# The output projection's first weight piece, cut in halves around the last values, in a decode attention kernel

## Chip, cores and metric

The kernel runs on one core of one Trainium2 chip. The metric is device time in microseconds (us) of one execution. Beside it stands one execution recorded by the hardware profiler; its span runs from the first to the last profiled instruction of the program.

## What is computed

One decode step for two tokens (B = 2, D = 512): a layer norm, grouped attention over the last 4096 positions of a cache, an output projection with `wo`, and a gate from a small gated MLP.

```python
xn = _layernorm(x)
# attention: 32 query heads, 8 key/value heads, Dh = 128, W = 4096
q = (xn @ wq).reshape(B, 1, 32, 128).transpose(0, 2, 1, 3)
k = repeat(k_cache[:, :, Sk - W:, :], 4, axis=1)
v = repeat(v_cache[:, :, Sk - W:, :], 4, axis=1)
p = softmax(einsum("bhqd,bhkd->bhqk", q, k) * Dh ** -0.5)
o = einsum("bhqk,bhkd->bhqd", p, v)
s = o.transpose(0, 2, 1, 3).reshape(B, 1, 4096) @ wo        # wo is 4096 x 512
# gate: gMLP with w_in, w_sp, b_sp, w_out
g = silu(_B_ref(xn, w_in, w_sp, b_sp, w_out))
return x + s * g
```

Everything is fp32. Nearly all of the time goes into reading the window of both caches (32 MB each, eight loads of 4 MB), `wq` and `wo` (8 MB each) and `w_in`.

## The kernel before

The 16 pairs of token and key/value head are worked on as eight **units** `u` = 0 to 7, each with two heads: units 0 to 3 belong to token 0, units 4 to 7 to token 1. A unit's keys `K:u` and values `V:u` are 4 MB each. Every load is issued on SP's queue. VectorE transposes the keys in eight turns (`T:u.q`); TensorE multiplies them with the queries (`shares`, `scores`), in two halves `a`; VectorE and ScalarE make the softmax (`rowmax`, `mg`, `bias`, `exp`, `probs_t`); TensorE multiplies the probabilities with the values (`pv:u.a`, which needs `V:u`), ScalarE evacuates (`evac`), TensorE and VectorE bring the heads into columns (`col`, `gather`).

The output projection takes three **sets** of heads, `SETS`: set 0 is key/value heads 0 to 3 (16 blocks of `wo`, 4 MB), set 1 is heads 4 and 5 (8 blocks, 2 MB), set 2 is heads 6 and 7 (8 blocks, 2 MB). A block is 128 rows by 512 columns of `wo`. Set 0 is complete when units 0, 1, 4 and 5 are gathered, set 1 after unit 6, set 2 after unit 7. `spread:i` (TensorE) and `oT:i` (VectorE, function `place`) turn a set's values into the stationary operand `oT_i`.

The blocks are multiplied in two ways. The first 28 blocks go through `wo_early`: 128 x 512 matmuls, one of four column groups of the array each, summed in the PSUM tile `part`; each fp32 matmul shows in the profile as two passes. ScalarE then copies `part` to SBUF (`parts`) and four small matmuls (`pz`, function `add_parts`) add its four groups into `so`. The last four blocks go through `wo_last`, straight into `so`, as four 128 x 128 matmuls each. VectorE multiplies `so` with the gate, adds `x`, and SP writes the output.

The order of all this is written out by hand in the string `ORDER`: each name is one step, taken from left to right, and each engine gets its instructions in that order. A step on an engine therefore stands behind all earlier steps of that engine, whatever they wait for. The loads `K`, `V`, `wo` stand in the same string and set the order of SP's queue. They go into a ring of four 4 MB buffers (`slot`), so a load is issued once the buffer's former content has been used: in the kernel before, `V:7` follows keys 6 (`T:6.7`), `wo:0` follows values 5 (`pv:5.1`), `wo:1` follows keys 7 (`T:7.7`).

In the kernel before, `wo:0` is one transfer of 4 MB. `wo:1` is one buffer filled by five transfers: 2 MB of set 1, then set 2 as 1 MB, 512 KB, 256 KB and 256 KB. In `ORDER`, `X:n` is two blocks of set 0, `Y:n` two blocks of set 1, `U:n` two of the first four blocks of set 2, and `Z:0`, `Z:1`, `Z:2` are the last 2, 1 and 1 blocks.

Of the kernel before, what the change touches and what calls it, by code (L numbers as in the profile page):

```python
# [9 lines left out]
F32 = mybir.dt.float32  # L10
# [4 lines left out]
P = 128  # L15
# [28 lines left out]
scores:5.1 evac:4 col:4 rowmax:5.0  # L44
K:7 V:6 T:6.0 rowmax:5.1 mg:5 T:6.1 T:6.2 shmax:5 bias:5 T:6.3 exp:5.0 T:6.4 exp:5.1 T:6.5 probs_t:5.0 shares:6.0
keep:6.0 lsum:5 shsum:5 scores:6.0 probs_t:5.1 T:6.6 T:6.7 rowmax:6.0 pv:5.0 weights:5 shares:6.1 keep:6.1 pv:5.1
V:7 T:7.0 wo:0 scores:6.1 rowmax:6.1 T:7.1 T:7.2 mg:6 T:7.3 shmax:6 bias:6 T:7.4 evac:5 col:5 exp:6.0 exp:6.1 T:7.5
probs_t:6.0 T:7.6 T:7.7 wo:1 lsum:6 shares:7.0 keep:7.0 pv:6.0 scores:7.0 shares:7.1 rowmax:7.0 keep:7.1 shsum:6
scores:7.1 probs_t:6.1 weights:6 rowmax:7.1 mg:7 pv:6.1 evac:6 shmax:7 gather:5 col:6 bias:7 exp:7.0 gather:6 exp:7.1
probs_t:7.0 spread:0 probs_t:7.1 lsum:7 spread:1 pv:7.0 shsum:7 oT:0 weights:7 pv:7.1 X:0.6 X:0.0 oT:1 X:0.2 X:0.4  # L50
evac:7 X:0.3 col:7 X:0.7 gather:7 spread:2 X:0.5 Y:0.1 Y:0.0 Y:0.3 X:0.1 Y:0.2 oT:2 U:0.0 U:0.1 parts:0 Z:0 pz:0 Z:1 Z:2
"""


# [16 lines left out]
def kernel(  # L71
# [14 lines left out]
    pe, dve, act, sp = (InOrder(tc, e) for e in (nc.tensor, nc.vector, nc.scalar, nc.sync))  # L86
    B, _, D = x.shape
# [11 lines left out]
    DC = D // G  # L99
# [9 lines left out]
    ps = ctx.enter_context(tc.tile_pool(name="ps", bufs=1, space=bass.MemoryType.PSUM))  # L109

    def slot(name, *shape):
        return ring.tile([P, *shape], F32, tag="slot", name=name)

    def bank(name, *shape):
        return ps.tile([P, *shape], F32, tag="kt", name=name, bufs=2)
# [11 lines left out]
    for a in range(0, KT, 2):  # L127
        t = slot(f"wq{a}", 2, HQ * DH)
# [17 lines left out]
    def load(u, src, name):  # L146
        t = slot(f"{name}{u}", UJ, DH)
        b, v = divmod(u, HKV // 2)
        first = src[b, 2 * v, SK - W, :]
        of = bass.AP(tensor=src.tensor, offset=first.offset, ap=[[UJ * DH, P // 2], [SK * DH, 2], [1, UJ * DH]])  # L150
        sp.dma_start(t.rearrange("p j d -> p (j d)"), of)
        return t
# [17 lines left out]
    rowm = cst.tile([P, 32], F32, tag="rowm", name="rowm")  # L170
# [55 lines left out]
    for nj in (8, 16):  # L226
# [3 lines left out]
        at = cst.tile([P, nx], F32, tag=f"at{nj}", name=f"at{nj}")  # L230
# [7 lines left out]
    for n in range(G):  # L238
        pz = bank(f"z{n}", 512)[:, :FC]
        for k in range(KT):  # L240
            pe.matmul(
                pz[32 * k : 32 * k + 32, :], xnT[:, k, :], win[:, k, n * FC : (n + 1) * FC],
                start=True, stop=True,
# [31 lines left out]
    u = cst.tile([P, 2, FT, B], F32, tag="u", name="u")  # L275
# [37 lines left out]
    for j in range(FT):  # L313
        g = j % G
# [26 lines left out]
    def place_queries():  # L341
        dve.tensor_tensor(
            free_ap(qb, 16, [[REP, G], [32, NP * G], [1, REP]]), free_ap(qa, 0, [[0, G], [REP, NP * G], [1, REP]]),
            free_ap(grpm, 0, [[1, G], [0, NP * G], [0, REP]]), op=ALU.mult,
        )
# [3 lines left out]
    def silu():  # L349
        dve.tensor_scalar(gate, ys, -1.0, 80.0, op0=ALU.mult, op1=ALU.min)  # L350
        act.activation(gate, gate, AF.Exp)
        dve.tensor_scalar_add(gate, gate, 1.0)
        dve.reciprocal(gate, gate)
        dve.tensor_mul(gate, gate, ys)
# [10 lines left out]
    sets = {}  # L365
    for i, (kv, n, nj) in enumerate(SETS):
        o1 = cst.tile([P, B, 32], F32, tag=f"o1_{i}", name=f"o1_{i}")
        oT = cst.tile([P, nj, 32], F32, tag=f"oT_{i}", name=f"oT_{i}")
# [102 lines left out]
    col = {}  # L471
# [22 lines left out]
    def spread(i):  # L494
        o1, oT, nj = sets[f"oT{i}"]
        pts[i] = bank(f"oT_ps{i}", B, 32)
        pe.matmul(pts[i], perms[nj][0].rearrange("p h a x -> p (h a x)"), o1, start=True, stop=True)

    def place(i):
        _, oT, nj = sets[f"oT{i}"]  # L500
        nx = 32 // nj
        t = sb.tile([P, B, nx, nj], F32, tag="ot", name=f"ot{i}", bufs=1)
        dve.tensor_tensor(
            t, pts[i].rearrange("p b (x j) -> p b x j", x=nx), free_ap(perms[nj][1], 0, [[0, B], [1, nx], [0, nj]]),
            op=ALU.mult,
        )
        dve.tensor_reduce(
            oT[:, :, 0 : 16 * B : 16].rearrange("p j b -> p b j"), t.rearrange("p b x j -> p b j x"), axis=AX.X, op=ALU.add
        )


    wo_s = []
# [2 lines left out]
        wo_s.append(wo[r0:r1, :].rearrange("(p j) d -> p j d", j=nj))  # L515
    blocks = []

    def load_wo(n):
        t = slot(f"wo{n}", 16, D)
        a = 0  # L520
        for i in ((0,), (1, 2))[n]:
            for j, n in (((0, 16),), ((0, 8),), ((0, 4), (4, 2), (6, 1), (7, 1)))[i]:
                sp.dma_start(t[:, a : a + n, :], wo_s[i][:, j : j + n, :])
                blocks.append((t[:, a : a + n, :], sets[f"oT{i}"][1], j))
                a += n

    EARLY = 28
    done = 0
# [1 line left out]
    def wo_early(n, at):  # L530
        nonlocal done
        if done == 0:
            part.append(ps.tile([P, 512], F32, tag="s0", name="part"))
        t, oT, j = blocks[n]
        for a in range(at, at + 2):
            g = done % G
            pe.matmul(
                part[0][32 * g : 32 * g + 32, :], oT[:, j + a, :], t[:, a, :], start=(done < G), stop=(done >= EARLY - G)
            )
            done += 1  # L540

    part = []

    def copy_parts():
        parts.append(sb.tile([P, D], F32, tag="o", name="parts", bufs=1))
        act.activation(parts[0], part[0], AF.Copy)

    def wo_last(n):
        if n == 0:
            so.append(bank("so", DC))  # L550
        t, oT, j = blocks[3 + n]
        for a in range(t.shape[1]):
            for g in range(G):
                pe.matmul(
                    so[0][32 * g : 32 * g + 32, :], oT[:, j + a, :], t[:, a, g * DC : (g + 1) * DC],
                    start=(n == 0 and a == 0), stop=(j + a == oT.shape[1] - 1),
                )

    def add_parts():
        for g in range(G):  # L560
            pe.matmul(
                so[0][32 * g : 32 * g + 32, :], rowm, parts[0][:, g * DC : (g + 1) * DC], start=False, stop=False
            )

    parts, so = [], []
    STEPS = dict(
        T=turn, rowmax=row_max, mg=spread_max, shmax=share_max, bias=bias, exp=probs, probs_t=probs_t, lsum=own_sum,
        shsum=share_sum, weights=weights, shares=shares, keep=keep, scores=scores, pv=pv, evac=evacuate, col=collect,
        gather=gather,
    )  # L570

    def step(name, u, a=()):
        if name == "q":
            place_queries()
        elif name == "silu":
            silu()
        elif name == "K":
            units[u].k = load(u, k_cache, "k")
        elif name == "V":
            units[u].v = load(u, v_cache, "v")  # L580
        elif name == "wo":
            load_wo(u)
        elif name == "spread":
            spread(u)
        elif name == "oT":
            place(u)
        elif name == "X":
            wo_early(0, 2 * a[0])
        elif name == "Y":
            wo_early(1, 2 * a[0])  # L590
        elif name == "U":
            wo_early(2, 2 * a[0])
        elif name == "Z":
            wo_last(u)
        elif name == "parts":
            copy_parts()
        elif name == "pz":
            add_parts()
        else:
            STEPS[name](units[u], *a)  # L600
# [6 lines left out]
    for line in ORDER.strip().split("\n"):  # L607
        for name in line.split():
            name, at = name.split(":")
            u, _, a = at.partition(".")  # L610
            step(name, int(u), (int(a),) if a else ())
# [33 lines left out]
```

## Time and profile before

| | |
|---|---|
| median of 3 runs | 217.01 us (216.76 to 217.04) |
| the profiled execution's own time | 217.29 us |
| its span | 215.5 us |
| mean granted TensorE clock | 0.825 |
| TensorE matmul busy | 143.2 us (66%) |
| VectorE busy | 126.7 us (59%) |
| ScalarE busy | 51.6 us (24%) |
| read from memory | 89.40 MB, 415 GB/s over the span |

A busy share is the part of the span in which the engine had an instruction running; matmul ends are modelled, so TensorE's share is not its load at its peak. Lines of the profile name an engine (PE is TensorE's matmul, PEld its weight load, DVE VectorE, ACT ScalarE, SPq SyncE's queue), the operation, and its output and inputs by tile names. Nearly all instructions carry line 65, the helper that keeps program order, so they are told apart by tile: `acc` is `pv`, `sh` is `shares`, `part` is `wo_early`, `so` is `wo_last` and `add_parts`.

### The profile page before, as it was taken

Reading aid. Unit: us, or ns where it says so; the run is one execution under the profiler, and the core shown is the slowest. Engines: PE = TensorE matmul, PEld = TensorE weight load, DVE = VectorE, ACT = ScalarE, POOL = GpSimd, SP = SyncE. Lnnn points to the kernel's source line nnn. Section 1 sums busy time; section 2 is a strip of 40 time slices with the busy share of each in tenths; the row PEclk is TensorE's granted clock in tenths of the full one; section 3 lists DMA queues with packets and bytes.
Section 4 is the critical chain, followed back from the end, with each engine's and each line's share of the span. In section 5 each row is a group of like instructions: output and inputs, shape, how many; then the busy total and the mean of one; then the engine's idle time right before and its main releaser. Section 6 shows DMA issues by size and latency. Waiting matters only on the chain.

```text
span 215.5 us, 2332 instructions
## 1 busy us (share of the span) xinstructions
PE 143.2 (66%) x900; PEld 48.1 (22%) x900; DVE 126.7 (59%) x218; ACT 51.6 (24%) x129; POOL 4.5 (2%) x17
## 2 busy tenths in 40 slices
PE   0179796833854966964991795389259917987793
PEld 0117622111120221222220231123112201232231
DVE  2611213169899799649928972993698099636011
ACT  5011103300116036033330602142051206142201
POOL 8000000000000000000000000000000000000000
PEclk9999569665998896796697599669755997996999
DMA  7999999999999999999999999999999999999990
GB/s 246 432 443 444 398 429 465 414 458 414 456 408 447 420 426 444 426 443 426 450 420 450 408 441 420 426 450 426 447 415 456 401 456 414 447 426 417 420 374 22
DMA packets 3930, 89.54 MB, mean 416 GB/s; under 512 B 446, under 2 KB 462, under 8 KB 848
## 3 DMA queue, kind: packets, MB, share of 16 engines
q1 hardware_dynamic: 3900, 89.40, 96.8%
q8 instruction: 7, 0.11, 0.2%
q14 instruction: 3, 0.02, 0.0%
q10 hardware_dynamic: 20, 0.01, 0.0%
HBM read 89.40 MB, written 0.00 MB: 415 GB/s over the span
## 4 chain that ended last, share of the span: by engine, by line
DMA 63%; PE 23%; DVE 8%; ACT 3%; issue 1%; ACTq 0%
DMA v<-in_A_v_cache_dram 42%; DMA k<-in_A_k_cache_dram 16%; PE acc L65 10%; DMA win<-in_B_w_in_dram 5%; PE sh L65 5%; DVE kts L65 4%; PE part L65 4%; PE s L65 3%; DVE pT L65 1%; ACT p L65 1%; ACT o L65 1%; DVE gate L65 1%; PE mo L65 1%; ACT ss L65 1%; DVE qb L65 1%
## 5 line engine op out<-in xcount | busy, mean ns | idle before, releaser
L65 DVE STREAM_TRANSPOSE kts<-k 128x1024 f32<-128x1024 f32 x64 | 75.6, 1218 | 29.5 <-DMA k<-in_A_k_cache_dram 29.5
L65 PE MATMUL sh<-kts,qb 128*32 128x512 f32 x256 | 41.6, 775 | 13.2 <-DVE kts L65 9.3
L65 PE MATMUL acc<-v,pT 128*32 128x512 f32 x256 | 37.4, 707 | 8.8 <-DVE pT L65 4.4
L65 ACT ACTIVATE p<-s,nb 128x512 f32<-128x512 f32 x32 | 22.5, 733 | 36.2 <-DVE nb L65 36.2
L65 ACT ACTIVATE ss<-sh 128x512 f32<-128x512 f32 x16 | 9.6, 599 | 59.1 <-PE sh L65 59.1
L65 DVE STREAM_TRANSPOSE pT<-p 128x1024 f32<-128x1024 f32 x16 | 19.6, 1225 | 2.3 <-ACT p L65 2.1
L65 PE MATMUL s<-ss,sums 128*128 128x512 f32 x32 | 18.8, 671 | 2.3 <-ACT ss L65 2.3
L65 PE MATMUL mo<-mg,joint 128*128 128x16 f32 x16 | 4.0, 327 | 23.4 <-DVE mg L65 23.4
L65 PEld LDWEIGHTS acc<-v,pT 128*32 128x32 f32 x256 | 10.5, 145 | 35.1 <-issue 27.0
L65 PEld LDWEIGHTS sh<-kts,qb 128*32 128x32 f32 x256 | 8.8, 126 | 34.2 <-issue 28.8
L65 DVE TENSOR_REDUCE m<-s 128x1 f32<-128x512 f32 x16 | 10.7, 671 | 4.2 <-PE s L65 4.2
L65 PE MATMUL q_ps<-wq,xnT 128*32 128x512 f32 x64 | 10.5, 784 | 3.5 <-DMA wq<-in_A_wq_dram 3.5
L65 ACT ACTIVATE o<-acc,wd 128x128 f32<-128x128 f32 x32 | 9.1, 368 | 15.0 <-PE acc L65 15.0
L65 PEld LDWEIGHTS mo<-mg,joint 128*128 128x128 f32 x16 | 3.2, 250 | 27.2 <-DVE mg L65 24.4
L65 PE MATMUL z<-win,xnT 128*32 128x448 f32 x32 | 5.6, 869 | 4.7 <-DMA win<-in_B_w_in_dram 4.7
L65 PE MATMUL part<-wo,oT 128*32 128x512 f32 x56 | 7.7, 596 | 1.4 <-ACT o L65 1.4
L65 PEld LDWEIGHTS s<-ss,sums 128*128 128x128 f32 x32 | 5.0, 197 | 10.3 <-issue 7.7
L65 PE MATMUL zT_ps<-rowm,z 128*128 128x2 f32 x28 | 6.6, 370 | 0.0
L65 PEld LDWEIGHTS zT_ps<-rowm,z 128*128 128x128 f32 x28 | 6.5, 325 | 0.0
L65 ACT ACTIVATION_READ_ACCUMULATOR p<-s,nb 128x1 f32 x32 | 6.5, 203 | 0.0
L65 ACT ACT_TABLE_LOAD x4 | 5.1, 1283 | 2.6 <-POOL hT L164 2.6
L65 DVE COPY z<-z 128x448 f32<-128x448 f32 x2 | 1.3, 626 | 7.5 <-PE z L65 7.5
(111 smaller groups left out, 68.4 us busy)
## 6 DMA issues: line engine op xcount, KB each, us to landing
k<-in_A_k_cache_dram SPq DMA_DIRECT2D x8, 4096.0 KB, 27.4
v<-in_A_v_cache_dram SPq DMA_DIRECT2D x8, 4096.0 KB, 29.8
wq<-in_A_wq_dram SPq DMA_DIRECT2D x1, 4096.0 KB, 24.5
wq<-in_A_wq_dram SPq DMA_DIRECT2D x2, 2048.0 KB
wo<-in_A_wo_dram SPq DMA_DIRECT2D x1, 4096.0 KB, 30.4
win<-in_B_w_in_dram SPq DMA_DIRECT2D x1, 3584.0 KB, 11.5
wo<-in_A_wo_dram SPq DMA_DIRECT2D x1, 2048.0 KB
wout<-in_B_w_out_dram SPq DMA_DIRECT2D x1, 1792.0 KB, 15.3
```

The lines of the kernel that those rows point to most:

```text
L65: return self.tc.keep_in_program_order(call(*args, **kwargs))
```

## The change

The first piece of `wo` is loaded in two halves of 2 MB, one ahead of `V:7` and one behind it. Set 2 comes in three transfers (4, 3 and 1 blocks) in place of four (4, 2, 1, 1). The first half's eight blocks (`X:0.0` to `X:0.3`) now stand between `col:6` and `pv:7.0`; for that, `gather:5`, `spread:0` and `oT:0` are moved ahead. The second half's eight blocks (`X:1.0` to `X:1.3`) stand behind `pv:7.1`. The tile `part` takes a buffer of the tag `acc` in place of the one of `s0`. `add_parts` now opens the sum in `so` and stands ahead of all of `wo_last`; there are two of those steps in place of three (3 blocks and 1 block).

```diff
 ORDER (the lines for the last two units)
-V:7 T:7.0 wo:0 scores:6.1 rowmax:6.1 T:7.1 T:7.2 mg:6 T:7.3 shmax:6 bias:6 T:7.4 evac:5 col:5 exp:6.0 exp:6.1 T:7.5
-probs_t:6.0 T:7.6 T:7.7 wo:1 lsum:6 shares:7.0 keep:7.0 pv:6.0 scores:7.0 shares:7.1 rowmax:7.0 keep:7.1 shsum:6
-scores:7.1 probs_t:6.1 weights:6 rowmax:7.1 mg:7 pv:6.1 evac:6 shmax:7 gather:5 col:6 bias:7 exp:7.0 gather:6 exp:7.1
-probs_t:7.0 spread:0 probs_t:7.1 lsum:7 spread:1 pv:7.0 shsum:7 oT:0 weights:7 pv:7.1 X:0.6 X:0.0 oT:1 X:0.2 X:0.4
-evac:7 X:0.3 col:7 X:0.7 gather:7 spread:2 X:0.5 Y:0.1 Y:0.0 Y:0.3 X:0.1 Y:0.2 oT:2 U:0.0 U:0.1 parts:0 Z:0 pz:0 Z:1 Z:2
+wo:0.0 V:7 wo:0.1 T:7.0 scores:6.1 rowmax:6.1 T:7.1 T:7.2 mg:6 T:7.3 shmax:6 bias:6 T:7.4 evac:5 col:5 exp:6.0 exp:6.1
+T:7.5 gather:5 probs_t:6.0 T:7.6 T:7.7 wo:1.0 wo:2.0 wo:2.1 wo:2.2 lsum:6 shares:7.0 keep:7.0 spread:0 pv:6.0 scores:7.0
+shares:7.1 rowmax:7.0 keep:7.1 shsum:6 oT:0 scores:7.1 probs_t:6.1 weights:6 rowmax:7.1 mg:7 pv:6.1 evac:6 shmax:7 col:6
+bias:7 exp:7.0 gather:6 X:0.0 X:0.1 exp:7.1 probs_t:7.0 X:0.2 X:0.3 probs_t:7.1 lsum:7 spread:1 pv:7.0 shsum:7 weights:7
+pv:7.1 oT:1 X:1.0 evac:7 X:1.1 col:7 X:1.2 gather:7 spread:2 X:1.3 oT:2 Y:0.0 Y:0.1 Y:0.2 Y:0.3 U:0.0 U:0.1 parts:0 pz:0
+Z:0 Z:1

-    def load_wo(n):
-        t = slot(f"wo{n}", 16, D)
-        a = 0
-        for i in ((0,), (1, 2))[n]:
-            for j, n in (((0, 16),), ((0, 8),), ((0, 4), (4, 2), (6, 1), (7, 1)))[i]:
-                sp.dma_start(t[:, a : a + n, :], wo_s[i][:, j : j + n, :])
-                blocks.append((t[:, a : a + n, :], sets[f"oT{i}"][1], j))
-                a += n
+    PIECES = (((0, 8), (8, 8)), ((0, 8),), ((0, 4), (4, 3), (7, 1)))
+    wo_t = {}
+
+    def load_wo(i, n):
+        if i < 2 and n == 0:
+            wo_t[i] = slot(f"wo{i}", 16, D)
+        t, at = (wo_t[i], 0) if i < 2 else (wo_t[1], 8)
+        j, count = PIECES[i][n]
+        sp.dma_start(t[:, at + j : at + j + count, :], wo_s[i][:, j : j + count, :])
+        blocks.append((t[:, at + j : at + j + count, :], sets[f"oT{i}"][1], j))

     def wo_early(n, at):
-            part.append(ps.tile([P, 512], F32, tag="s0", name="part"))
+            part.append(ps.tile([P, 512], F32, tag="acc", name="part", bufs=2))

     def wo_last(n):
-        if n == 0:
-            so.append(bank("so", DC))
-        t, oT, j = blocks[3 + n]
+        t, oT, j = blocks[4 + n]
...
-                    start=(n == 0 and a == 0), stop=(j + a == oT.shape[1] - 1),
+                    start=False, stop=(j + a == oT.shape[1] - 1),

     def add_parts():
+        so.append(bank("so", DC))
         for g in range(G):
             pe.matmul(
-                so[0][32 * g : 32 * g + 32, :], rowm, parts[0][:, g * DC : (g + 1) * DC], start=False, stop=False
+                so[0][32 * g : 32 * g + 32, :], rowm, parts[0][:, g * DC : (g + 1) * DC], start=True, stop=False
             )
```

(`step` passes the new numbers on: `wo:i.n` to `load_wo(i, n)`, `X:u` to block group `u`, `Y` to group 2, `U` to group 3.)

More of the change, by code (lines that the diff above doesn't have):

```diff
@@ L581, in step @@
         elif name == "wo":
-            load_wo(u)
+            load_wo(u, a[0])
         elif name == "spread":
@@ L587, in step @@
         elif name == "X":
-            wo_early(0, 2 * a[0])
+            wo_early(u, 2 * a[0])
         elif name == "Y":
-            wo_early(1, 2 * a[0])
+            wo_early(2, 2 * a[0])
         elif name == "U":
-            wo_early(2, 2 * a[0])
+            wo_early(3, 2 * a[0])
         elif name == "Z":
```

## The prediction, on record before the change was run

> **What bounds the kernel now.** I read first the transfer rows of the page's slices, because a kernel that reads 89 MB may have nothing else to lose time to.
>
> ```profile
> DMA  7999999999999999999999999999999999999990
> GB/s 246 432 443 444 398 429 465 414 458 414 456 408 447 420 426 444 426 443 426 450 420 450 408 441 420 426 450 426 447 415 456 401 456 414 447 426 417 420 374 22
> ```
>
> From the second slice to the last but one the transfer engines are 90% busy or more. A change that moves the same bytes can win only behind the last transfer, or where TensorE does not keep up with it. So the second view is the chain of waits over the last 35 us (start, length, what).
>
> ```profile
> 150.21 32.33 DMA v<-in_A_v_cache_dram
> ...
> 193.99 1.26 DVE pT L65
> 195.24 0.04 issue
> 195.29 3.27 PE acc L65 x16
> 198.55 0.31 PE mo L65 x2
> 198.87 1.93 PE acc L65 x16
> ...
> 200.87 1.15 ACT o L65 x4
> 202.02 0.09 issue
> 202.11 2.05 PE part L65 x17
> ...
> 206.95 3.64 PE part L65 x28
> ...
> 210.68 0.61 ACT parts L65
> 211.28 0.04 issue
> 211.33 0.93 PE so L65 x24
> ```
>
> Read alone, this is TensorE's tail: the last unit's values (195.29), 28 blocks of `wo` (from 202.11), the copy, the last sum (to 212.26). It invites the thought that eight blocks done earlier shorten the tail. The third view asks when the pieces of `wo` land (issues on SP's queue in three windows: the first piece, and the last one).
>
> ```profile
> L65 SPq DMA_DIRECT2D wo<-in_A_wo_dram x1: 337/337/337, 171.6 to 171.6; - x1
> ...
> DMA to landing us min/median/max: 30.4/30.4/30.4
> ...
> L65 SPq DMA_DIRECT2D wo<-in_A_wo_dram x1: 431/431/431, 186.0 to 186.0; - x1
> ...
> DMA to landing us min/median/max: 25.7/25.7/25.7
> ```
>
> The first piece lands at 171.6 + 30.4 = 202.0, and TensorE's first `part` matmul starts at 202.11: the chain blames ScalarE's `o`, whose end at 202.02 is a coincidence. The last piece lands at 186.0 + 25.7 = 211.7. Values 6 landed at 150.21 + 32.33 = 182.54, so 8 MB (values 7 and the first piece) took 202.0 - 182.5 = 19.5, or 9.73 for 4 MB, and the last 4 MB, five pieces, 211.7 - 202.0 = 9.7. Counting back and forth with that pace: values 7 landed at 192.3, set 1's 2 MB at 206.9, the 1 MB of set 2 at 209.3. Now TensorE's weight loads at the end (start, length, idle before):
>
> ```profile
> 206.92 0.19 PEld L65 LDWEIGHTS part<-wo,oT 128*32 128x32 f32 x8 [0.91 <-issue]
> 207.38 0.15 PEld L65 LDWEIGHTS part<-wo,oT 128*32 128x32 f32 x4 [0.27 <-issue]
> ...
> 209.37 0.30 PEld L65 LDWEIGHTS part<-wo,oT 128*32 128x32 f32 x8 [0.56 <-issue]
> 210.58 0.41 PEld L65 LDWEIGHTS so<-wo,oT 128*32 128x32 f32 x16 [0.91 <-PE part L65]
> 211.33 0.16 PEld L65 LDWEIGHTS so<-parts,rowm 128*32 128x32 f32 x8 [0.34 <-ACT parts L65]
> 211.46 0.48 PEld L65 LDWEIGHTS so<-wo,oT 128*32 128x32 f32 x16
> ```
>
> Set 1 begins at 206.92 (landed 206.9, idle 0.91 before), set 2 at 209.37 (landed 209.3, idle 0.56 before). So **TensorE waits for a landing at each piece**, and whatever it does earlier is forgotten at the next one. The last time it is brought into step is 209.3. From there to 212.26 runs a chain that the change edits too.
>
> **The change part by part.** The sum is made against the profiled execution, 217.29 us with a span of 215.5; the median of the runs shown is 217.01, and the difference found is carried over to it.
>
> *Halves and their place in the queue.* Bytes and number of transfers stay (six before, six now). The 4 MB that went in five pieces took 9.7, the 4 MB that went in one 9.73, so I take the new cuts at nothing, within 0.1 either way. The queue has no gap for a late issue to widen: in the last rows a transfer waits 25 to 30 us between issue and landing, so an issue that comes some us later is hidden, and would cost only what exceeded that. On SP the first half takes the place and buffer of `V:7` (issued when keys 6 are used), and `V:7` with the second half behind it the place of `wo:0` (171.6, when values 5 are used). Landings then are: first half 182.5 + 4.9 = 187.4, values 7 at 197.1 (192.3 before), second half 202.0, the rest as now.
>
> *Eight blocks moved.* A pair of blocks is four passes, and 207.38 - 206.92 = 0.46 or less, so eight blocks are 1.8. They leave the stretch behind 202.11 and go between `col:6` and `pv:7.0`, where TensorE waits until 195.29. Their half landed at 187.4, so they wait for nothing there. Behind 202.11 the work until set 1 is shorter by 1.8, but set 1 still lands at 206.9: worth nothing. The moved `gather:5`, `spread:0` and `oT:0` come some us earlier, on VectorE ahead of two transpositions; whatever they push back is covered until values 7 land.
>
> *Values 7 later.* `pv:7.0` waits until 197.1 instead of 195.29, 1.8 more; queued behind it on TensorE are the row sum, `pv:7.1`, the second half's blocks, `col:7`, `spread:2`; on ScalarE `evac:7`. At the pace of now (3.27 + 0.31 + 1.93) the values end at 202.6, the evacuation (1.15) at 203.8; eight blocks, `col:7`, the gather and `spread:2` take TensorE and VectorE some 3 more, to about 206.8. Set 1 lands at 206.9. Cover: the pause in front of set 1, and behind that the 2.4 to set 2. Cost nothing.
>
> *The end, from 209.3 on.* This is where I find a cost. Before, `part` was finished at 210.59; during ScalarE's copy (210.68 to 211.28) TensorE did the first two of the last four blocks, the 16 passes at 210.58, for nothing. Then came 24 passes from 211.33: eight of `pz` and eight for each of two blocks, 0.93 in all; less the last pass's own 0.27 that is 0.66, 0.22 for eight.
>
> ```profile
> L65 PE MATMUL so<-wo,oT x32: 269/273/297, 210.6 to 211.9; 128*32 128x128 f32 x32
> ```
>
> Now `add_parts` opens the sum, so nothing can stand beside the copy: behind it come `pz`, three blocks, one block, 40 passes, 5 x 0.22 + 0.27 = 1.37. That is 0.44 more. Against it: set 2's eight passes now start on an idle array. Before, 209.37 to 210.59 was 1.2; idle starts show a second group 0.46 behind the first (206.92 and 207.38), and one pass lasts 0.59, so 1.05 to 1.1: 0.1 gained. The sum is +0.34, or +0.44 if the idle array gains nothing. I take +0.4, with the cuts' 0.1 either way.
>
> ```profile
> L65 PE MATMUL part<-wo,oT x56: 589/592/617, 202.1 to 210.0; 128*32 128x512 f32 x56
> ```
>
> The last landing doesn't add to this: at 211.7 the last block's weights are there, and TensorE will come to that block only at 211.3 + 4 x 0.22 = 212.2. So the end passes from the landing to TensorE. Sum: 217.29 + 0.4 = 217.7 for the profiled execution, and on the median of runs 217.01 + 0.4 = **217.4**. A measurement of this kernel can tell about 0.2%, 0.43 us, from no change; the forecast lies just inside that, and its own bounds (+0.2 to +0.6) on both sides.
>
> **The clock, weighed against the skill.** Granted clock by stretch of 3.4 us (length, TensorE busy with its count, clock, transfers):
>
> ```profile
> 191.21:194.63 3.42, 1.72 (x18) 1.00 0.95 412
> 194.63:198.04 3.41, 2.75 (x16) 0.50 0.96 413
> 198.04:201.45 3.41, 2.71 (x26) 1.00 0.95 408
> 201.45:204.87 3.42, 2.76 (x32) 1.00 0.96 410
> 204.87:208.28 3.41, 3.00 (x28) 1.00 0.99 413
> 208.28:211.69 3.41, 3.31 (x50) 1.00 0.53 205
> ```
>
> Behind a stretch with TensorE busy 1.72 of 3.42 the clock was halved for the next; that is why the first `pv` took 3.27 and the second 1.93. The Trainium skill, page "TensorE: Matmul & The Clock Gate", section "Part 1: The HAM clock gate", has the clock fall to half only after at least one idle window of about 3.4 us. By that rule no pause of the changed kernel would halve it, and the sum stays at 217.4. The trace doesn't agree: 1.72 us of work did not hold the clock.
>
> **The rivals.**
>
> *The clock halves at the end* (slower). The eight blocks taken out leave a pause in front of set 1: if values 7 run at full clock (two times 1.93 from 197.1), everything before set 1 is done by about 204.9, and TensorE is idle for 2.0, then busy 1.7 with set 1, then idle 0.7 until set 2. A stretch that begins near 204 or 204.9 would hold 1.4 or so of work, less than the 1.72 above. For it: that row. Against: it depends on how the stretches fall, and where values 7 run at half clock there is no such pause. It decides if the halved stretch covers 209.4 to 210.5. Price: set 2's passes take 1.07 more at most, part of the last sum 0.1 to 0.3: +0.9 to +1.3 on top of +0.4, about 218.5.
>
> *The transfer engines end evenly* (faster). In the last stretch they are busy 0.53 of 3.41: filled evenly they would have ended at 208.28 + 1.81 = 210.1, not 211.4 to 211.7. If the new cuts or their place happened to spread the late engines' load, set 2 would land up to 1.3 earlier: 217.4 - 1.3 = 216.1. It decides from 0.85 on, where it exceeds cost and measurement. For it: the row. Against: the cuts share the same rows out in the same way.
>
> *The last landing sets the end* (no change). If the 24 passes of the last two steps overlap the copy or run at half of 0.22, TensorE is at the last block by 211.7 and the end stays: 217.0. Against it: `add_parts` opens the sum and stands ahead.
>
> *Values 7 come too late* (slower). If values 7 land over 2.4 behind 197.1, or both `pv` run at half clock (3.27 each) and the rest slips too, set 2 begins late by the excess; at 1 us, 218.4. Against it: the cover worked out above.
>
> **How the numbers follow.** Forecast 0.57, of which 0.27 falls over +0.43, 0.29 within and 0.01 below; clock 0.20; even engines 0.08; last landing 0.08; late values 0.07. Faster 0.09, same 0.37, slower 0.54. The predicted time is the forecast's, 217.4. The range leaves out the even engines and the upper end of the clock's price: 216.9 to 218.5. The forecast's own range is 217.2 to 217.6.
>
> **What would show it.** Right: `part` begins near 193, `pv:7.0` near 197.1; idle in front of set 1's loads near 206.9; set 2's loads near 209.4; 40 passes into `so` in one run of about 1.4 behind `parts`, and no pass into `so` during the copy. The span is longer by about 0.4, all of it behind the copy. Wrong: `part`'s last passes at the half clock (the clock rival); transfers done before 210.5 (even engines); a wait in front of the last block (the landing sets it); set 2's loads later than 209.6 with no idle before (late values).

## The result, and the profile after

The changed kernel takes 217.19 us (median of 14 runs, 216.98 to 217.82) against 216.85 (216.74 to 217.04): slower by 0.34 us, ratio 1.0017, 95% interval 1.0010 to 1.0023. Its profiled execution took 216.98, span 215.2; that is one of its fastest, so the two profiles' spans are not to be subtracted. What can be compared is the stretch behind one and the same landing. The chain of waits at the end of the changed kernel (start, length, what):

```profile
184.25 24.39 DMA wo<-in_A_wo_dram
208.63 0.14 issue
208.77 1.10 PE part L66 x8
209.87 0.02 issue
209.89 0.02 ACTq L66
209.91 0.04 issue
209.95 0.60 ACT parts L66
210.56 0.04 issue
210.60 1.34 PE so L66 x40
```

The chain now goes straight from a landing (set 2's 1 MB, at 208.63) into the end: eight passes, the copy, and 40 passes into `so` in one run of 1.34. No pass into `so` stands beside the copy; TensorE's weight loads say the same:

```profile
206.31 0.19 PEld L66 LDWEIGHTS part<-wo,oT 128*32 128x32 f32 x8 [2.34 <-issue]
...
208.74 0.19 PEld L66 LDWEIGHTS part<-wo,oT 128*32 128x32 f32 x8 [1.39 <-issue]
...
210.60 0.16 PEld L66 LDWEIGHTS so<-parts,rowm 128*32 128x32 f32 x8 [1.68 <-ACT parts L66]
210.74 0.90 PEld L66 LDWEIGHTS so<-wo,oT 128*32 128x32 f32 x32
```

Before, set 2's loads began at 209.37 and `so` was done at 212.26: 2.89. Now 208.74 and 210.60 + 1.34 = 211.94: 3.20. The difference is 0.31, nearly the whole loss of 0.34. In front of set 1 TensorE's weight loads idle for 2.34 (0.91 before), in front of set 2 for 1.39 (0.56 before): the time that the eight early blocks set free is spent waiting. Where those blocks went, and values 7:

```profile
192.34 1.90 PE L66 MATMUL part<-wo,oT 128*32 128x512 f32 x16
...
196.65 1.95 PE L66 MATMUL acc<-v,pT 128*32 128x512 f32 x16 [2.04 <-DMA v<-in_A_v_cache_dram]
```

### The profile page after: what moved, and what is told of

The parts are those of the page before. It is cut to its first block, busy times and chain, and to the rows that moved or that the text cites. A ratio compares the mean times of both kernels' runs of the same rounds, so it can differ in the third digit from the quotient of the medians.

```text
span 215.2 us, 2330 instructions
## 1 busy us (share of the span) xinstructions
PE 140.7 (65%) x900; PEld 47.4 (22%) x900; DVE 126.6 (59%) x218; ACT 51.7 (24%) x129; POOL 4.5 (2%) x17
## 4 chain that ended last, share of the span: by engine, by line
DMA 68%; DVE 24%; PE 3%; ACT 3%; issue 1%; SPq 0%; ACTq 0%
DMA k<-in_A_k_cache_dram 51%; DVE kts L66 18%; DMA wo<-in_A_wo_dram 11%; DMA win<-in_B_w_in_dram 5%; DVE pT L66 2%; ACT p L66 2%; PE sh L66 2%; DVE m L66 1%; DVE gate L66 1%; PE so L66 1%; DVE nb L66 1%; PE s L66 1%; DVE qb L66 1%; PE part L66 1%; ACT parts L66 0%
## 5 line engine op out<-in xcount | busy, mean ns | idle before, releaser
L66 PE MATMUL acc<-v,pT 128*32 128x512 f32 x256 | 35.3, 672 | 9.4 <-DMA v<-in_A_v_cache_dram 6.5
L66 PE MATMUL s<-ss,sums 128*128 128x512 f32 x32 | 19.4, 692 | 2.3 <-ACT ss L66 2.3
L66 PE MATMUL q_ps<-wq,xnT 128*32 128x512 f32 x64 | 10.0, 756 | 2.8 <-DMA wq<-in_A_wq_dram 2.8
```

The lines of the kernel that those rows point to most:

```text
L66: return self.tc.keep_in_program_order(call(*args, **kwargs))
```

## The experiments

All times are medians, with the ratio to the kernel before on the same chips and its 95% interval. The kernel before stood at 216.86 to 216.88 in all of them.

**The end alone, and everything but the end.** Two runs split the change. The first puts the old end back:

```diff
-    PIECES = (..., ((0, 4), (4, 3), (7, 1)))
+    PIECES = (..., ((0, 4), (4, 2), (6, 1), (7, 1)))
-parts:0 pz:0 Z:0 Z:1
+parts:0 Z:0 pz:0 Z:1 Z:2      # and Z:0 opens so again
```

> The changed kernel with the old end put back (set 2 as 4, 2, 1 and 1 blocks, the first two of the last blocks multiplied during the copy, the sum opened by them); halves, values 7 between them and the eight early blocks stay. Theory 'the end' (16 passes that now stand behind the copy cost the 0.34 us): the cost is gone, 216.85 +- 0.1, same as before. Theory 'values 7' (the cut and the later values cost it): stays at 217.2. Theory 'the early blocks are worth something, and the end hides it': faster than before by 0.2 or more, 216.6 or below.

Measured: 217.05, ratio 1.0012 (1.0004 to 1.0021). Between the two expectations: some of the 0.34 goes away, 0.19 stays, and the interval overlaps that of the changed kernel (1.0010 to 1.0023), so this run alone does not show the end to be the cause. In its profile, that of its slowest execution (217.53), the first two of the last four blocks stand beside the copy again, and the last block waits for the last landing:

```profile
209.29 0.19 PEld L66 LDWEIGHTS part<-wo,oT 128*32 128x32 f32 x8 [1.38 <-issue]
210.53 0.41 PEld L66 LDWEIGHTS so<-wo,oT 128*32 128x32 f32 x16 [1.06 <-PE part L66]
211.15 0.16 PEld L66 LDWEIGHTS so<-parts,rowm 128*32 128x32 f32 x8 [0.21 <-ACT parts L66]
211.29 0.24 PEld L66 LDWEIGHTS so<-wo,oT 128*32 128x32 f32 x8
211.79 0.16 PEld L66 LDWEIGHTS so<-wo,oT 128*32 128x32 f32 x8 [0.26 <-DMA wo<-in_A_wo_dram]
```

The second puts the new end alone into the kernel before:

```diff
-            for j, n in (..., ((0, 4), (4, 2), (6, 1), (7, 1)))[i]:
+            for j, n in (..., ((0, 4), (4, 3), (7, 1)))[i]:
-parts:0 Z:0 pz:0 Z:1 Z:2
+parts:0 pz:0 Z:0 Z:1          # and add_parts opens so
```

> The kernel before with only the new end (set 2 as 4, 3 and 1 blocks, the sum opened by the copied part, three blocks and one block behind it); the first piece of wo is whole, no block is moved. Theory 'the end': 216.85 + 0.3 to 0.45, about 217.2, and 40 passes into so in one run of about 1.4 us behind the copy; a bit more than the changed kernel, as set 2's passes still start on a busy array. Theory 'values 7': no difference, 216.85.

Measured: 217.43, 1.0025 (1.0016 to 1.0034), 0.57 slower. The end costs by itself, and more than within the whole change and than expected: in its profile set 2's loads begin at 208.72 and the 40 passes run from 210.74 for 1.34, so 3.37 in place of 2.89, since set 2's passes still queue behind set 1's. In this execution values 7 began only at 197.02 and at the half clock (3.54), and its chain has no landing from there on, so some of the 0.57 may be that lateness.

**Which edit of the end.** Order and pieces were changed together. One run keeps the new order with the old four pieces, one keeps the new pieces with the old order.

```diff
 # g3: pieces 4, 2, 1, 1 as before          # g4: pieces 4, 3, 1 as changed
+parts:0 pz:0 Z:0 Z:1 Z:2                   +parts:0 Z:0 pz:0 Z:1
```

> The changed kernel with set 2 again in four transfers (4, 2, 1, 1 blocks); pz still opens the sum behind the copy, so all four last blocks stand behind it. Theory 'the end' (what counts is that 16 passes stand behind the copy): as the changed kernel, 217.2 +- 0.15. If it is the piece of three blocks that costs, through its later landing: 216.95.

> The changed kernel with its three transfers of set 2 (4, 3, 1 blocks), but the three blocks ahead of pz, as far as they landed, and opening the sum. Theory 'the end': the three blocks land only about when the copy is done, so nothing stands beside the copy here either, pz waits behind the three blocks, and the end is that of the changed kernel, 217.15 +- 0.15. If the order alone costs: 216.95.

Measured: 217.36, 1.0023 (1.0014 to 1.0032), and 217.25, 1.0019 (1.0010 to 1.0028). Either edit is enough for the whole loss. In the second the three blocks land at 210.77, when the copy (210.27 to 210.87) is all but done, so nothing stands beside the copy here either, and `pz` waits behind them:

```profile
185.03 25.74 DMA wo<-in_A_wo_dram
210.77 0.14 issue
210.91 1.33 PE so L66 x40
```

From set 2's loads to the end of `so` the profiles fall into two groups. With the cut and either new edit of the end it is 3.18 to 3.21 (the changed kernel, these two runs, and the one without the second half below). With the old end it is 2.87 to 2.97 (the kernel before in two profiles, the old end put back, and the runs with eight blocks left out and with the rehearsal below).

**Is there any slack at the end?** The three blocks are multiplied twice.

```diff
-parts:0 pz:0 Z:0 Z:1
+parts:0 pz:0 Z:0 Z:0 Z:1
```

> The changed kernel with the three blocks behind pz multiplied twice (24 passes into so more; their products count double in the output). Theory 'the end lies on TensorE with no slack': 24 x 0.0275 = 0.66 more, 217.19 + 0.66 = 217.85. Theory 'the last landing still sets the end': up to 0.3 of it hidden, 217.5 or less.

Measured: 217.94, 0.75 over the changed kernel, ratio to before 1.0049 (1.0036 to 1.0062). In its profile the run into `so` takes 0.66 more, 2.00 for 64 passes:

```profile
208.79 0.14 issue
...
210.76 2.00 PE so L66 x64
```

So TensorE sets the end with no slack, and a pass there costs 0.0275.

**Are the early blocks worth anything?** Eight of set 0's blocks are left out of the kernel before.

```diff
-    EARLY = 28
+    EARLY = 20
-pv:7.1 X:0.6 X:0.0 oT:1 X:0.2 X:0.4
+pv:7.1 oT:1
```

> The kernel before with eight of set 0's blocks left out (a quarter of the output projection is missing), nothing moved. Theory 'TensorE waits for a landing at each piece': 1.8 us less work in front of set 1 is worth nothing, 216.86, at most 0.1 faster. The view of a tail of TensorE: 1.7 us faster, 215.1. If values 7 at the half clock make TensorE late in some executions: 0.1 to 0.3 faster in the median.

Measured: 216.90, 1.0005 (0.9994 to 1.0016). Behind the old order of loads, 1.8 us less work on TensorE is worth nothing. One of the twelve executions took 218.28, the others 216.75 to 217.09; what happened in that one is not in a trace.

**What the cut does alone.** From the first run's kernel, the eight early blocks go back behind the values, and `gather:5`, `spread:0` and `oT:0` to their old places; halves and the later values 7 are all that is left.

```diff
-gather:6 X:0.0 X:0.1 exp:7.1 probs_t:7.0 X:0.2 X:0.3 probs_t:7.1
+gather:6 exp:7.1 probs_t:7.0 spread:0 probs_t:7.1
-pv:7.1 oT:1 X:1.0 evac:7
+pv:7.1 X:0.0 X:0.1 oT:1 X:0.2 X:0.3 X:1.0 evac:7
```

> The first run's kernel with all 16 blocks of set 0 behind the values of unit 7, as before; only the halves and values 7 between them are left of the change. Theory 'the end': landings catch up by set 2, 216.85 +- 0.1; set 1's passes may begin up to 1 us behind its landing, without effect. Theory 'values 7': 217.1 or more, since eight blocks (1.8 us) more stand between values 7 and set 1.

Measured: 217.72 (216.99 to 218.02; two of the six executions below 217.3), 1.0034 (1.0021 to 1.0047). The time is that of theory 'values 7', and theory 'the end' failed: it costs 0.67 more than with the blocks moved. The chain shows TensorE busy from values 7 to the end, and no landing in it:

```profile
199.90 0.85 PE acc L66 x4
200.75 0.52 PE mo L66 x2
201.27 2.13 PE acc L66 x16
203.40 2.57 PE part L66 x24
205.98 0.22 PE col L66 x8
206.19 0.85 PE part L66 x4
207.05 0.36 PE oT_ps L66 x2
207.41 3.58 PE part L66 x28
```

Values 7 end at 203.40 in place of 200.80 before. Part of that is the clock, by stretches of 3.4 us (TensorE busy, clock):

```profile
191.58:195.00 3.42, 1.27 (x13) 1.00 0.94 407
195.00:198.40 3.40, 1.30 (x8) 0.50 0.96 410
198.40:201.82 3.42, 3.42 (x18) 0.50 0.97 417
```

Behind the pause in which TensorE waits for values 7 the clock is halved for them. Is it the clock, or the eight blocks of work? One run does both: the eight blocks in the pause, as a rehearsal whose sum is overwritten, and again behind the values.

```diff
 # against e1_old_end; D multiplies X's blocks into part without counting them
-gather:6 X:0.0 X:0.1 exp:7.1 probs_t:7.0 X:0.2 X:0.3 probs_t:7.1
+gather:6 D:0.0 D:0.1 exp:7.1 probs_t:7.0 D:0.2 D:0.3 probs_t:7.1
-pv:7.1 oT:1 X:1.0 evac:7
+pv:7.1 X:0.0 X:0.1 oT:1 X:0.2 X:0.3 X:1.0 evac:7
```

> The kernel with the old end and the cut, where the eight early blocks are multiplied twice: once where the change puts them, as a rehearsal whose result is overwritten, and again behind the values of unit 7. The run with halves alone took 217.72 against 217.05 with the early blocks. Theory 'clock': its excess came from values 7 at the half clock (6.8 us of half clock over 195 to 201.8), and work in the pause before them keeps the clock: 217.1 +- 0.15. Theory 'amount of work': eight blocks more between values 7 and set 1 are what costs: 217.6 or more, as with halves alone.

Measured: 217.09, 1.0008 (1.0000 to 1.0017). With all 16 blocks behind the values again, but the clock kept, the loss against the run with the old end (217.05) is gone:

```profile
191.60:195.00 3.40, 2.51 (x26) 1.00 0.93 400
195.00:198.40 3.40, 1.58 (x16) 1.00 0.93 400
198.40:201.82 3.42, 3.42 (x34) 1.00 1.01 431
```

The two runs also differ in the place of `gather:5`, `spread:0` and `oT:0`, which stay early in the rehearsal; that place does not delay the values, since `pv:7.0` starts 14.5 us after `pv:6.0` in both profiles. So the early blocks' worth beside the cut is that they keep TensorE's clock, not that they are done. They do not keep it always, as the next run shows.

**A pause in front of set 1.** The prediction's clock rival: the second half's blocks are left out of the changed kernel, so that the pause before set 1 grows.

```diff
-    EARLY = 28
+    EARLY = 20
-oT:1 X:1.0 evac:7 X:1.1 col:7 X:1.2 gather:7 spread:2 X:1.3 oT:2
+oT:1 evac:7 col:7 gather:7 spread:2 oT:2
```

> The changed kernel without the second half's eight blocks (a quarter of the output projection is missing), so that TensorE has only the columns and the spread to do between values 7 and set 1, a pause of about 4 us or more. Theory 'a pause halves the clock': a stretch with under 1.4 us of work out of 3.4 is followed by a half clock, set 2 or the last sum fall into it in some executions, 0.5 to 1.3 us slower than the changed kernel in those, 217.6 or more in the median. If no halved stretch reaches set 2: 217.2 as the changed kernel, as the missing work was done in a wait.

Measured: 216.92, 218.06, 218.24 and 218.78, median 218.15; ratio 1.0067 (1.0052 to 1.0083). Less work, and 0.9 to 1.6 slower in three of four executions. The profiled one is the 216.92. Up to values 7 it does the same work as the changed kernel, with the eight early blocks in the pause, and yet its clock was halved over values 7. Here the whole pause in front of `pv:7.0` (194.6 to 196.6) lay in one stretch:

```profile
193.86:197.27 3.41, 1.37 (x14) 1.00 0.87 375
197.27:200.68 3.41, 3.41 (x18) 0.50 0.99 423
```

The clock is whole from there to the end, and the end is the changed kernel's own (208.72 for the first of set 2's passes, `so` done at 211.90). That the slow ones had the clock halved later is therefore inferred from the times, not seen in a trace. Over all profiles, values 7 ran at a whole clock in seven of the eight with work from `wo` in the pause, and in one of the six without.

**A shorter chain behind set 2.** If the copy is on the way, move it ahead of set 2. Once with the early blocks (from the changed kernel), once without (from the kernel before).

```diff
-    PIECES = (..., ((0, 4), (4, 3), (7, 1)))      # in both: set 2 as 5, 2, 1 blocks
+    PIECES = (..., ((0, 5), (5, 2), (7, 1)))
-    EARLY = 28
+    EARLY = 24
-U:0.0 U:0.1 parts:0 pz:0 Z:0 Z:1
+parts:0 pz:0 Z:0 Z:1 Z:2
```

> The changed kernel with part closed after set 1 (24 blocks), so that its copy and its sum lie in the pause before set 2 lands, and set 2 in pieces of 5, 2 and 1 blocks multiplied straight into so. Theory 'the end': between the landing of set 2's first piece and the last landing TensorE has only 56 passes (1.55 us) in place of a copy and 48 passes, so the last landing sets the end: one block (0.45 us) behind it, 0.3 to 0.4 us faster than the changed kernel, 216.8 +- 0.1, and not over 0.1 faster than before, whose last block began 0.04 after its landing. Theory 'values 7': stays at 217.2.

> The kernel before (first piece whole, behind values 7; all 16 blocks of set 0 behind the values) with part closed after 24 blocks, and set 2 in pieces of 5, 2 and 1 blocks straight into so. Theory 'the last landing sets the end once no copy stands behind set 2': 216.8 +- 0.1, the last block's passes begin within 0.1 of the last landing. A rival, 'TensorE's own queue sets the end of the kernel before': with values 7 at the half clock set 2 begins late and the gain is over 0.2 in the median, 216.6.

Measured: with the early blocks 216.95, 1.0003 (0.9994 to 1.0011); without them 217.38, 1.0027 (1.0016 to 1.0039). The first came out as expected in its mechanism, and 0.24 faster than the changed kernel where 0.3 to 0.4 was expected: the copy is done by 208.94, and the last block's loads wait for the last landing.

```profile
208.99 0.16 PEld L66 LDWEIGHTS so<-parts,rowm 128*32 128x32 f32 x8 [1.68 <-ACT parts L66]
209.30 1.58 PEld L66 LDWEIGHTS so<-wo,oT 128*32 128x32 f32 x56 [0.15 <-issue]
211.11 0.16 PEld L66 LDWEIGHTS so<-wo,oT 128*32 128x32 f32 x8 [0.23 <-DMA wo<-in_A_wo_dram]
```

The second missed: without the early blocks, 20 passes stand behind set 1's landing, `part` is finished only at 209.34, and copy and 72 passes come after set 2 has landed.

```profile
206.56 2.78 PE part L65 x20
...
209.42 0.61 ACT parts L65
210.03 0.04 issue
210.07 2.22 PE so L65 x72
```

The run with the early blocks is 0.43 faster here. Whether that is because they are done is not shown: four of the 20 passes are set 0's `X:0.1`, which `ORDER` has behind `Y:0.3`, while the weight loads idled for 0.89 in front of set 1, and no run moved them ahead. No version was shown to beat the kernel before.

**How executions differ.** The kernel before once more, for its profile.

> The kernel before, unchanged, for a second profile. The last landing was at 211.7 in its first profile and at 211.1 in that of the changed kernel, with the same bytes and the same last pieces. If that is how executions differ, this one has some other last landing between 211.0 and 211.8, and the stretch from set 2's landing to the end of so is again 3.0 us, against 3.3 in the changed kernel.

Measured: 216.79. Weight loads and the last row of its chain:

```profile
208.86 0.30 PEld L65 LDWEIGHTS part<-wo,oT 128*32 128x32 f32 x8 [0.56 <-issue]
...
210.81 0.95 PE so L65 x24
```

Set 2's loads begin 0.51 earlier than in its first profile, the end comes 0.50 earlier (211.76), and the stretch is 2.90, against 2.89. Landings differ between executions of the same program by over half a microsecond; the stretch behind one doesn't.

## Why the prediction held

The forecast was 217.4 and slower; measured 217.19 and slower by 0.34, inside its own range of 217.2 to 217.6 but for 0.01. The cost was found where it was forecast, behind set 2's landing. Point by point:

*Landings bound the end of the kernel before*: shown, though not for every execution. Leaving eight blocks out gave 216.90 against 216.88, and the idle time of the weight loads grew by 1.43 in front of set 1 and by 0.83 in front of set 2. But in the profile of the new end alone, with the old order of loads, the chain has no landing behind values 7.

*The copy with nothing beside it*: shown. It is the larger part of the loss. Forecast +0.34 to +0.44, taken as 0.4. The traces give 0.31 (3.20 against 2.89); 40 passes took 1.34, forecast 1.37. By medians of runs, the three with the cut and a new end (217.19, 217.36, 217.25) lie 0.24 above the three with the cut and an end that waits for the last landing (217.05, 217.09, 216.95). That the last landing no longer sets the end is shown by the three blocks multiplied twice, which cost their full 0.66. The term was sized a little too high in the idle array: set 2's eight passes took 1.10 (1.2 before), so the 0.1 that I had worked out was gained, and I had counted half of it. The reason was too narrow: I blamed `add_parts` opening the sum; the piece of three blocks alone does the same.

*The cut at nothing, within 0.1*: not shown. Those last three lie 0.17 above the kernel before on average; their intervals run from -0.13 to +0.46 and none excludes 0.1. The traces do not show a delay: from the start of `pv:6.0`, which waits for values 6 to land, to set 2's loads it is 26.56 to 26.69 in four profiles without the cut and 26.60 to 26.76 in five with it. Where the 0.17 comes from stays open; if it is real, part of the agreement of 0.4 with 0.34 is luck, since the forecast had this term at nothing.

*Values 7 later, at nothing*: right for the changed kernel, but for a reason that I had not seen. I had put the cover in the pause before set 1; without the early blocks the cover doesn't hold (217.72), and what comes is the rival *Values 7 come too late*. With them the clock stayed whole in the changed kernel's profile, `pv:7.0` ran in 1.95 in place of 3.27, and `col:7` was done by 202.7. The eight blocks, which I had priced at nothing, pay for the delay that the cut makes.

*The clock*: in the changed kernel the stretches with 2.14, 2.18 and 2.10 us of work held a whole clock:

```profile
195.37:198.79 3.42, 2.14 (x18) 1.00 0.96 412
...
205.61:209.03 3.42, 2.18 (x20) 1.00 0.99 416
209.03:212.44 3.41, 2.10 (x48) 1.00 0.27 105
```

and those with 1.72 (before), 1.37 (without the second half) and 1.27 (halves alone) were followed by a halved one. The Trainium skill, page "TensorE: Matmul & The Clock Gate", section "Part 1: The HAM clock gate", has the clock fall after at least one idle window of about 3.4 us; these rows don't agree with that, a stretch half idle was enough. The busy time alone does not decide either: in the rehearsal a stretch with 1.58 was followed by a whole clock, and in the second profile of the kernel before one with 1.95 (192.33 to 195.74) by a halved one. So the prediction's reading of its row, that less than 1.72 loses the clock, is too simple. The clock rival did not decide here: none of 14 executions came near 218.5; its price, +0.9 to +1.3, is of the size that the run with the longer pause shows (0.9 to 1.6). Whether the one execution at 217.82 is such a case is open.

*The transfer engines ending evenly* did not come: the last landing moved between executions (211.7, 211.1) without the change.

## What to carry to other kernels

Find the last landing that TensorE really waits for, and count only what stands between it and the end; work taken out from ahead of it turns into idle time. A reduction that is opened by one step or another decides what can stand beside a copy: let the part that already landed open it. When a transfer is moved ahead of another, ask what keeps TensorE's clock up until the delayed one lands.

## What was not expected of the hardware

That doing 16 useless passes in a pause can make a kernel faster: they took 0.63 us off the median (217.72 to 217.09), with the same matmuls behind the pause. In the two profiles a stretch with 1.27 us of work in 3.42 was followed by a halved clock and one with 2.51 was not. And the last transfers of the same program land over half a microsecond apart from one execution to the next (the kernel before: set 2's loads at 209.37 and at 208.86), which is more than the change under study was worth.
